# mLSTM cell and feed-forward on one core: the cell visits of two steps placed together in chunks 2 to 5

## The chip, the core and the metric

The kernel runs on one core of a Trainium2 chip. The metric is the device time of one execution in microseconds (us). The profile is that of one further execution, with the start, length and cause of waiting of each instruction on each engine: PE is TensorE (matmuls), DVE is VectorE, ACT is ScalarE, POOL is GpSimd, SP is the queue that issues nearly all DMAs.

## What is computed

Inputs are q, k, v and an output gate of 4 batches, 8 heads, 768 time steps and 40 features, and two gates per time step. The recurrence over time, and the feed-forward block on its result, are:

```python
m_new = np.maximum(f_gate[:, :, t] + m, i_gate[:, :, t])
f_stab = np.exp(f_gate[:, :, t] + m - m_new)
i_stab = np.exp(i_gate[:, :, t] - m_new)
C = f_stab[:, :, None, None] * C + i_stab[:, :, None, None] * np.einsum('bhd,bhe->bhde', vt, kt)
n = f_stab[:, :, None] * n + i_stab[:, :, None] * kt
h_tilde = np.einsum('bhde,bhe->bhd', C, qt)
denom = np.maximum(np.abs(np.einsum('bhd,bhd->bh', n, qt)[:, :, None]), 1.0)
y[:, :, t] = o * h_tilde / denom          # o is the sigmoid of the output gate
...
h = x @ w_in                              # x: y as (3072 tokens, 320); w_in: 320 x 2048
g = np.maximum(0.01 * h, h)
out = g @ w_out                           # w_out: 2048 x 320
```

All data are fp32 in the kernel.

## The kernel before

**Tiling.** Time is cut into 6 chunks of 128 time steps (`NB`). A *step* `s` is one chunk of one batch, all 8 heads: `s = 4c + b`, 24 steps in all. Inside a step the chunk is computed in closed form as two sub-chunks of 64 time steps: products of k and q, weighted by exponentials of the gates (`w`), plus the contribution of the state that the earlier sub-chunk left. The feed-forward block of chunk `c-1` (512 tokens of the four batches) runs while the cell of chunk `c` is computed.

**Feed-forward units.** `ff_units(g)` (L734) gives 32 units for a chunk. Units 0 to 15 are eight pairs `j` of *first* and *second* (L753, L757): 6 and then 4 matmuls into two PSUM tiles `ph`, 64x128 weights on 512 tokens; *second* ends with two relus on ScalarE (L748), which write `acts`. Units 16 to 31 are `part(n, m)` (L771): 4 matmuls into `po`; every fourth unit ends with a copy of `po` on ScalarE (L783) and a DMA to the output. `ph` and `po` share one PSUM pool, `psf`, of four buffers (tag `mm`), so two pairs `j` can be open at once. The profile counts an fp32 matmul as two records.

**Cell visits.** In chunks 2 to 5 a step has two visits on TensorE. `u_parts(s)` (L579) runs what is left of the step's exponentials, then the joint products `sd` of k with q and of k with the values (L595, L600) into two PSUM tiles; VectorE multiplies them by `w` (L605) and adds to the state (L577). `u_mix(s)` (L665) starts with the gate's tanh on ScalarE (L475), then multiplies state and values with the weighted products into `pT` (L676). Behind it GpSimd scales the state (L573), VectorE transposes `pT` (L683), forms denominators (L614 to L616) and gates (L687), GpSimd divides (L690), VectorE adds to the state (L577) and transposes to `x` (L694), and four DMAs write `x` to DRAM (L697). `gather_x(s)` (L700) later reads it back as `xT`, the input of the next chunk's `ph`. `sd`, `pT` and the gate transposes `tg` (`u_gates`, L796) share the PSUM pool `psc`, four buffers (tag `c`).

**Preparation.** `ahead(s)` (L814) registers the step's eight exponentials in `lazy` (`prep_exp`, L433; each masks out the future in place, in `w`), queues transposes of k and q and a product with a gate factor on VectorE (`prep_kq`, L481: L486, L492), issues ten DMAs of step `s+2` on SP (`rb`, L382; `ea`, L405), and queues on GpSimd the state's scaling (L573), `vu` (L459) and the mask of step `s+1` (`prep_mask`, L429: L431), which adds minus infinity to the future entries of `w` and must come before that step's exponentials. For chunk 1, `ahead` also has TensorE transposes (`u_split`).

**The order of the work.** It is written out by hand: TensorE, VectorE, ScalarE and GpSimd execute in the order in which the code calls (`tc.manual_schedule`, L915); only SP's queue is ordered by the compiler. In the loop over a chunk's units (L940), each turn first runs three exponentials of every step in `lazy`, then the feed-forward unit `i`, then the cell units that are due:

```python
upto = sum(p <= i for p in place) if c == 1 else min(n_c, (i + 1) * n_c // (n_ff - 8))
while done < upto:
    fn, s = cells[done]
    fn(s)
    ...
    if fn in ((u_mix, u_plain) if s < 2 * B - 1 else (u_parts,)):
        ahead(s + 1)
```

In chunks 2 to 4 (nine cell units) this places `u_parts` and `u_mix` of the four steps in turn behind units 2, 5, 7, 10, 13, 15, then the gates of the next chunk behind unit 18, and the last step behind units 21 and 23. In chunk 5 (eight cell units) they stand behind units 2, 5, 8, 11, 14, 17, 20 and 23. `ahead(s+1)` follows `u_parts(s)` from step 7 on. Gathers are held back to unit 15, since `xT` has one buffer. Behind a `u_mix`, the feed of later steps is issued on SP: the gate of step `s+2`, and k, v and `w` of step `s+4` (L974 to L976).

In chunk 1 (`place`, L931) the steps have `u_plain` (L637) in place of `u_mix`, `u_x` (L714) puts `x` into `xT` by TensorE transposes and five ScalarE copies each, and the weights are still being narrowed from 64 bits by VectorE and ScalarE (`narrow_weights`).

Of the kernel before, what the change touches and what calls it, by code (L numbers as in the profile page):

```python
# [18 lines left out]
def kernel(  # L19
# [27 lines left out]
    B, H, S, D = q.shape  # L47
# [3 lines left out]
    NS = B * NB  # L51
# [86 lines left out]
    def subs(s):  # L138

        for u in range(2):  # L140
            yield u, ts(u, SL), slice(SL * (1 - u), SL * (1 - u) + D)
# [78 lines left out]
    def narrow_weights(n):  # L220

        if not wide:
            return
        raw, dst = raws.pop(n)
        words = raw.bitcast(U32).rearrange("p (c two) -> p c two", two=2)
        lo, hi = words[:, :, 0], words[:, :, 1]
        d = dst.bitcast(U32)
        low, top = lo.bitcast(F32), hi.bitcast(F32)  # L230
        nc.scalar.activation(dst, top, AF.Abs)
        yield
        nc.vector.tensor_scalar(
            dst, dst, scalar1=2.0**-15, scalar2=122879.9921875, op0=ALU.max, op1=ALU.min,
        )
        yield
        nc.vector.tensor_scalar(
            d, d, scalar1=0x07FFFFFF, scalar2=3, op0=ALU.bitwise_and, op1=ALU.logical_shift_left,
        )
        yield  # L240
        nc.vector.scalar_tensor_tensor(d, in0=hi, scalar=0xC0000000, in1=d, op0=ALU.bitwise_and, op1=ALU.bitwise_or)  # L241
        yield
        nc.vector.tensor_scalar(hi, d, scalar1=0xFF800000, scalar2=None, op0=ALU.bitwise_and)  # L243
        yield
        nc.vector.scalar_tensor_tensor(low, in0=lo, scalar=2.0**-52, in1=top, op0=ALU.mult, op1=ALU.mult)  # L245
        yield
        nc.vector.tensor_tensor(dst, dst, low, op=ALU.add)  # L247
# [108 lines left out]
    def natural(s, i):  # L356

        t = rb_t[s % NR][:, i]
        return t[:, : H * D].rearrange("p (h d) -> p h d", d=D)

    def load_late(s, i):

        if B <= s < 2 * B:
            if i > 0:
                c, b = divmod(s, B)
                nc.sync.dma_start(natural(s, i), (k, q, o_gate)[i][b, :, ts(c, P), :].rearrange("h p d -> p h d"))
        elif s < NS:
            load_blocks(s, i)
# [58 lines left out]
                )  # L427

    def prep_mask(s):  # L429
        w = st[s]["w"]  # L430
        nc.gpsimd.tensor_tensor(w, w, cm2.unsqueeze(1).to_broadcast([P, H, SL]), op=ALU.add)  # L431

    def prep_exp(s):  # L433

        c, b = divmod(s, B)
        w = st[s]["w"]
        for h in range(H):
            bh = b * H + h
            yield nc.scalar.activation(w[:, h, :], w[:, h, :], AF.Exp, bias=gT[c][:, 0, bh : bh + 1], scale=1.0)  # L439
# [23 lines left out]
    def prep_qs(s):  # L463

        c, b = divmod(s, B)
        d = st[s]
        d["qs"] = wk.tile([P, Dm], F32, name="y")[:].rearrange("p (h d) -> p h d", d=D)
        nc.gpsimd.tensor_tensor(
            d["qs"], natural(s, 1), gT[c][:, 2, ts(b, H)].unsqueeze(2).to_broadcast([P, H, D]), op=ALU.mult,
        )  # L470
# [10 lines left out]
    def prep_kq(s):  # L481

        d = st[s]
        d["kqT"] = wk.tile([P, 2, PR * P], F32, name="kqT")
        for i in range(2):
            nc.vector.transpose(  # L486
                d["kqT"][:, i].rearrange("p (h t n) -> p h n t", n=TS, t=QW),
                raw_blocks(s, i, QW).rearrange("p (h n) d -> p h n d", n=TS),
            )
        for r in range(2):  # L490
            rows = ts(r, SL)
            nc.vector.tensor_tensor(  # L492
                mixed(s)[rows, 1 - r], d["kqT"][rows, 1].rearrange("p (h t) -> p h t", t=SL), d["ea"][rows], op=ALU.mult,
            )
# [10 lines left out]
    def u_split(s):  # L505

        d = st[s]
        d["kqT"] = wk.tile([P, 2, PR * P], F32, name="kqT")
        src = (d["k"], natural(s, 1))
        bank = [psc.tile([P, H, SL], F32, name=f"tk{r}", tag="c") for r in range(2)]  # L510
        for h in range(H):
            for i in range(2):
                for u, toks, rows in subs(s):
                    out_rows = rows if i == 0 else slice(SL * u, SL * u + D)
                    nc.tensor.matmul(
                        bank[u][out_rows, h, :], lhsT=src[i][toks, h, :D], rhs=ident[toks, toks], start=True, stop=True,
                    )
        for i in range(2):
            for u, toks, rows in subs(s):
                out_rows = rows if i == 0 else slice(SL * u, SL * u + D)  # L520
                nc.scalar.copy(d["kqT"][rows, i].rearrange("p (h t) -> p h t", t=SL), bank[u][out_rows])
# [275 lines left out]
        gates_T(c, bus.pop(c)[0])  # L797

    def cell_units(c):
        units = [(fn, c * B + n) for n in range(B) for fn in (u_parts, u_mix if c > 1 else u_plain)]  # L800
        if c + 1 < NB:
            units.insert(2 * B - 2, (u_gates, c + 1))
        if c == 1:
            units += [(u_x, s) for s in range(B, 2 * B)]
        return units

    lazy = {}

# [5 lines left out]
    def ahead(s):  # L814

        if s < NS:
            if s < 2 * B:
                u_split(s)
            lazy[s] = prep_exp(s)
            if s < 2 * B:  # L820
                prep_qs(s)
            else:
                prep_kq(s)
            if s + NR < NS:
                load_late(s + NR, 0)
                load_late(s + NR, 1)
                if s + NR >= 2 * B:
                    spread_q(s + NR)
            state_next(s, 0)
            prep_vu(s)  # L830
            if s + 1 < NS:
                prep_mask(s + 1)

    def feed(s):
        load(s)
        spread(s)
# [78 lines left out]
    with tc.manual_schedule(engines={E.PE, E.DVE, E.Activation, E.Pool}):  # L915
        ffs = first_chunk()
        for s in (B, B + 1):
            feed(s)
            for i in range(1, 3):
                load_late(s, i)  # L920
            if s == B:
                load_weights(3)
        for n in range(3):
            load_weights(QN + n)
        for s in (B + 2, B + 3):
            feed(s)


        ffs = ffs[2:]
        fetch = {4: (3, 4), 8: (5, 6), 15: (7,)}  # L930
        place = (2, 5, 7, 10, 12, 15, 16, 18, 21, 22, 24, 26, 28)  # L931
        now = (None for n in range(2, QN + NF // 2) for _ in narrow_weights(n))
        for c in range(1, NB + 1):
            if c > 1:
                ffs = ff_units(c - 1)
            cells = cell_units(c) if c < NB else []
            n_ff, n_c = len(ffs), len(cells)
            done = fed = 0
            waiting = []
            for i in range(n_ff):  # L940
                if c == 1:
                    run(now, 2 if i < 10 else 3 if i < 14 else 4)
                    for n in fetch.get(i, ()):
                        load_weights(QN + n)
                    if i == 0:
                        prep_mask(B)
                        ahead(B)
                        load_fi(3)
                for steps in lazy.values():
                    run(steps, 3)  # L950
                ffs[i]()
                if c + 1 < NB:
                    if i == (1 if c == 1 else 0):
                        gates(c + 1)
                    if i == (3 if c == 1 else 2):
                        gates_exp(c + 1)
                upto = sum(p <= i for p in place) if c == 1 else min(n_c, (i + 1) * n_c // (n_ff - 8))
                while done < upto:
                    fn, s = cells[done]
                    fn(s)  # L960
                    done += 1
                    if fn is u_mix:
                        waiting.append(s)
                    if fn in ((u_mix, u_plain) if s < 2 * B - 1 else (u_parts,)):
                        ahead(s + 1)
                if i >= n_ff // 2 - 1:
                    for s in waiting:
                        gather_x(s)
                    waiting.clear()
                while fed < done:  # L970
                    fn, s = cells[fed]
                    fed += 1
                    if fn in (u_mix, u_plain):
                        load_late(s + NR, 2)  # L974
                        if s + NL < NS:
                            feed(s + NL)  # L976
# [31 lines left out]
```

## Time and profile before

| | |
|---|---|
| median of 3 runs | 534.39 us (533.99 to 534.42) |
| the profiled execution's own time | 533.48 us |
| its span, first to last instruction | 531.7 us |
| mean granted TensorE clock | 0.98 of full speed |
| busy, share of the span: PE, PEld | 97%, 63% |
| busy: DVE, ACT, POOL | 45%, 32%, 21% |
| L740 `ph`: records, busy | 1120, 217.3 us |
| L775 `po`: records, busy | 768, 213.3 us |
| L595 and L600 `sd`: busy | 23.0 and 20.6 us (they overlap) |
| L676 `pT`: records, busy | 512, 18.4 us |
| L439 exponentials on ACT: count, busy | 192, 52.5 us |
| L431 masks on POOL: count, mean | 20, 1333 ns |

How to read it: busy time of TensorE is modelled and overlapping, so the order and start times of its pieces say more than the sums. The *chain of work* is followed back from the last instruction; each piece in it is what the next one waited for. A timeline line gives start (us from the span's beginning), length (us), engine, line, operation, output and inputs, shapes, count; in brackets, the idle time in front of it and what ended that. Times of GpSimd are rough.

### The profile page before, as it was taken

To read this page: it belongs to the slowest core of one execution; us is meant where nothing else is said; L and a number is where in the kernel's file an instruction comes from. 1 tells how busy PE (TensorE), PEld (TensorE's weight loads), DVE (VectorE), ACT (ScalarE), POOL (GpSimd) and SP (SyncE) were. 2 spreads that over 40 slices of the span, in tenths; PEclk is the share of its full clock that TensorE was granted. 3 is DMA by queue.
4 is the path that set the end of the run, shared out by engine and by line. 5 is a ranking of instruction groups with operands and counts; after the bars stand their busy time and mean duration, and the time that the engine had idled before them with its cause. 6 is when DMAs were issued, how large, how long until landed. Compare 5 with 4: busy or idle time off the path is not lost.

```text
span 531.7 us, 11350 instructions
## 1 busy us (share of the span) xinstructions
PE 517.3 (97%) x4501; PEld 334.5 (63%) x4501; DVE 241.1 (45%) x431; ACT 168.0 (32%) x458; POOL 111.1 (21%) x145
## 2 busy tenths in 40 slices
PE   7879989999999999999999999999999999999997
PEld 7767878667545577545577555577555577544675
DVE  4788998999055526055616055614054432000000
ACT  4566767515434311134311134311134300122100
POOL 4245254153022223022223012323011100000000
PEclk9768999999999999999999999999999999999999
DMA  9977677878745647555547555546531221000000
GB/s 116 161 205 161 146 185 183 185 143 175 157 92 114 125 121 162 120 119 112 125 132 146 131 114 102 130 136 151 123 73 39 66 71 43 32 1 0 14 12 25
DMA packets 165284, 59.13 MB, mean 111 GB/s; under 512 B 128816, under 2 KB 156016, under 8 KB 165232
## 3 DMA queue, kind: packets, MB, share of 16 engines
q1 hardware_dynamic: 164848, 58.28, 50.2%
q8 instruction: 35, 0.57, 0.4%
q10 hardware_dynamic: 384, 0.13, 0.1%
q14 instruction: 17, 0.14, 0.1%
HBM read 51.68 MB, written 6.70 MB: 110 GB/s over the span
## 4 chain that ended last, share of the span: by engine, by line
PE 81%; DVE 7%; SPq 6%; DMA 2%; ACT 2%; issue 1%; POOL 1%; ACTq 0%; DVEq 0%; POOLq 0%
PE po L775 36%; PE ph L740 36%; PE pT L676 3%; SPq L213 3%; PE sd L595 3%; SPq L338 2%; DVE raw L245 1%; SPq L352 1%; PE sd L600 1%; DVE qn L605 1%; DVE w_out L247 1%; DMA rb<-in_q_dram 1%; DVE w_out L241 1%; DVE raw L243 1%; DMA raw<-in_moe_w_in_dram 1%
## 5 line engine op out<-in xcount | busy, mean ns | idle before, releaser
L740 PE MATMUL ph<-xT,w_in 64*128 64x512 f32 (+1 forms) x1120 | 217.3, 538 | 0.6 <-ACT acts L748 0.6
L775 PE MATMUL po<-w_out,acts 128*128 128x320 f32 x768 | 213.3, 435 | 0.0
L775 PEld LDWEIGHTS po<-w_out,acts 128*128 128x128 f32 x768 | 143.8, 190 | 59.7 <-issue 1.8
L740 PEld LDWEIGHTS ph<-xT,w_in 64*128 64x128 f32 x1120 | 107.1, 189 | 91.1 <-issue 84.4
L748 ACT ACTIVATE acts<-ph 128x512 f32<-128x512 f32 (+1 forms) x112 | 53.9, 534 | 145.6 <-PE ph L740 145.5
L605 DVE TENSOR_TENSOR qn<-w,sd 64x512 f32<-64x512 f32 x40 | 27.4, 686 | 125.6 <-PE sd L600 90.1
L573 POOL TENSOR_TENSOR S<-S,f 40x336 f32<-40x336 f32 x36 | 30.7, 854 | 187.8 <-PE pT L676 146.8
L439 ACT ACTIVATE w<-w,gT 128x64 f32<-128x64 f32 (+1 forms) x192 | 52.5, 351 | 1.0 <-DVE w L425 1.0
L783 ACT COPY y<-po 128x320 f32<-128x320 f32 x12 | 5.1, 426 | 86.6 <-PE po L775 86.6
L783 ACT COPY hn<-po 128x320 f32<-128x320 f32 x12 | 5.1, 427 | 86.3 <-PE po L775 86.3
L690 POOL TENSOR_TENSOR xb<-xb,den 128x320 f32<-128x320 f32 x16 | 11.7, 729 | 88.9 <-DVE xb L687 88.9
L431 POOL TENSOR_TENSOR w<-w,i 128x512 f32<-128x512 f32 x20 | 26.7, 1333 | 10.2 <-DMA w<-a_dr 10.1
L683 DVE STREAM_TRANSPOSE hb<-pT 128x512 f32<-128x512 f32 x16 | 11.5, 717 | 38.1 <-PE pT L676 38.1
L595 PEld LDWEIGHTS sd<-kqT 40*64 40x64 f32 x640 | 20.3, 135 | 10.8 <-issue 9.3
L595 PE MATMUL sd<-kqT 40*64 40x64 f32 x640 | 23.0, 221 | 0.0
L492 DVE TENSOR_TENSOR qn<-kqT,ea 64x512 f32<-64x512 f32 x32 | 22.4, 701 | 1.1
L676 PEld LDWEIGHTS pT<-qn,S 128*64 128x64 f32 x512 | 16.2, 138 | 10.5 <-issue 6.9
L600 PE MATMUL sd<-S,vu 64*40 64x42 f32 x576 | 20.6, 215 | 0.7 <-POOL vu L459 0.7
L694 DVE STREAM_TRANSPOSE x<-xb 128x512 f32<-128x512 f32 x16 | 17.6, 1102 | 8.0 <-POOL xb L690 8.0
L486 DVE STREAM_TRANSPOSE kqT<-rb 128x512 f32<-128x512 f32 x32 | 20.7, 682 | 0.0
L600 PEld LDWEIGHTS sd<-S,vu 64*40 64x40 f32 x576 | 18.2, 111 | 0.8 <-POOL vu L459 0.8
L577 DVE TENSOR_TENSOR S<-S,sd 40x336 f32<-40x336 f32 x36 | 18.1, 503 | 0.9
(126 smaller groups left out, 369.1 us busy)
## 6 DMA issues: line engine op xcount, KB each, us to landing
w<-a_dr SPq DMA_DIRECT2D x40, 128.0 KB
rb<-in_k_dram SPq DMA_DIRECT2D x64, 80.0 KB
rb<-in_q_dram SPq DMA_DIRECT2D x64, 80.0 KB
rb<-in_o_gate_dram SPq DMA_DIRECT2D x64, 80.0 KB
ea<-a_dr SPq DMA_DIRECT2D x32, 128.0 KB
kn<-in_k_dram SPq DMA_DIRECT2D x24, 160.0 KB
raw<-in_moe_w_out_dram SPq DMA_DIRECT2D x6, 640.0 KB
S<-in_v_dram SPq DMA_DIRECT2D x80, 40.0 KB
```

The costliest lines, as they stand in the source:

```text
L431: nc.gpsimd.tensor_tensor(w, w, cm2.unsqueeze(1).to_broadcast([P, H, SL]), op=ALU.add)
L439: yield nc.scalar.activation(w[:, h, :], w[:, h, :], AF.Exp, bias=gT[c][:, 0, bh : bh + 1], scale=1.0)
L486: nc.vector.transpose(d["kqT"][:, i].rearrange("p (h t n) -> p h n t", n=TS, t=QW), raw_blocks(s, i, QW).rearrange("p (h n) d -> p h n d", ...
L492: nc.vector.tensor_tensor(mixed(s)[rows, 1 - r], d["kqT"][rows, 1].rearrange("p (h t) -> p h t", t=SL), d["ea"][rows], op=ALU.mult,)
L573: nc.gpsimd.tensor_tensor(new, old, g, op=ALU.mult)
L595: nc.tensor.matmul(bank[1 - u][toks, h, :], lhsT=kqT[rows, 0, ts(h, SL)], rhs=kqT[rows, 1, ts(h, SL)], start=True, stop=True,)
L600: nc.tensor.matmul(dC[u][:, h].rearrange("p k d -> p (k d)"), lhsT=d["ku"][toks, h], rhs=S_v[s % NL][toks, u, h, :, :V1], start=True, stop ...
L605: nc.vector.tensor_tensor(mixed(s)[toks, u], w[toks], bank[1 - u][toks], op=ALU.mult)
L676: nc.tensor.matmul(pT[DP * r : DP * (r + 1), j * P + u * SL : j * P + (u + 1) * SL], lhsT=S[:, u, h, :], rhs=m[:, u, h, :], start=True, st ...
L740: nc.tensor.matmul(ph[r][:, cols], lhsT=w_row(r, slot, j), rhs=xT[DP * r : DP * (r + 1), slot, cols], start=(slot == 0), stop=(slot == KC ...
L748: nc.scalar.activation(acts[:, f, cols], ph[r][:, cols], AF.Prelu, alpha=0.01)
L775: nc.tensor.matmul(po[n][:], lhsT=acts[:, f, ts(n, P)], rhs=w_out[:, f, :], start=(f == 0), stop=(f == NF - 1),)
```

## The change

In chunks 2 to 5 the order of the cell units becomes `u_parts(s)`, `u_parts(s+1)`, `u_mix(s)`, `u_mix(s+1)` for two steps at a time. A hand-written list places them: the first pair's parts behind unit 2 and its mixes behind unit 6, the second pair's parts behind unit 14, and gates and the second pair's mixes behind unit 19. `ahead(s+2)` now follows each `u_mix(s)` (and `ahead(9)` follows the last `u_plain` of chunk 1). From step 8 on the mask of a step is queued at the head of its own `ahead`, not at the tail of the `ahead` before. Chunk 1's own order of units stays.

```diff
     def prep_mask(s):
+        if s in masked:
+            return
+        masked.add(s)
         w = st[s]["w"]
...
     def cell_units(c):
-        units = [(fn, c * B + n) for n in range(B) for fn in (u_parts, u_mix if c > 1 else u_plain)]
+        if c == 1:
+            units = [(fn, c * B + n) for n in range(B) for fn in (u_parts, u_plain)]
+            units.insert(2 * B - 2, (u_gates, c + 1))
+            return units + [(u_x, s) for s in range(B, 2 * B)]
+        units = [(fn, c * B + n + m) for n in range(0, B, 2) for fn in (u_parts, u_mix) for m in range(2)]
         if c + 1 < NB:
             units.insert(2 * B - 2, (u_gates, c + 1))
-        if c == 1:
-            units += [(u_x, s) for s in range(B, 2 * B)]
         return units
...
             if s < 2 * B:
                 u_split(s)
+            if s > B:
+                prep_mask(s)
             lazy[s] = prep_exp(s)
...
             state_next(s, 0)
             prep_vu(s)
-            if s + 1 < NS:
+            if s + 1 < 2 * B:
                 prep_mask(s + 1)
...
+        pairs = (2, 2, 6, 6, 14, 14, 19, 19, 19)
...
-                upto = sum(p <= i for p in place) if c == 1 else min(n_c, (i + 1) * n_c // (n_ff - 8))
+                upto = min(n_c, sum(p <= i for p in (place if c == 1 else pairs)))
...
-                    if fn in ((u_mix, u_plain) if s < 2 * B - 1 else (u_parts,)):
+                    if fn is u_plain and s < 2 * B - 1 or fn is u_parts and s == 2 * B - 1:
                         ahead(s + 1)
+                    elif fn is u_mix or fn is u_plain:
+                        ahead(s + 2)
```

More of the change, by code (lines that the diff above doesn't have):

```diff
@@ L799, in cell_units @@
     def cell_units(c):
-        units = [(fn, c * B + n) for n in range(B) for fn in (u_parts, u_mix if c > 1 else u_plain)]
+        if c == 1:
[3 more added lines that the diff above has]
+        units = [(fn, c * B + n + m) for n in range(0, B, 2) for fn in (u_parts, u_mix) for m in range(2)]
         if c + 1 < NB:
             units.insert(2 * B - 2, (u_gates, c + 1))
-        if c == 1:
-            units += [(u_x, s) for s in range(B, 2 * B)]
         return units
+    masked = set()
     lazy = {}
```

## The prediction

> **What bounds the kernel now.** I read the page's chain of work first, then the chain in order of time, then the timelines of the four engines around one visit.
>
> ```profile
> PE 81%; DVE 7%; SPq 6%; DMA 2%; ACT 2%; issue 1%; POOL 1%; ACTq 0%; DVEq 0%; POOLq 0%
> PE po L775 36%; PE ph L740 36%; PE pT L676 3%; SPq L213 3%; PE sd L595 3%; SPq L338 2%; DVE raw L245 1%; SPq L352 1%; PE sd L600 1%; DVE qn L605 1%; DVE w_out L247 1%; DMA rb<-in_q_dram 1%; DVE w_out L241 1%; DVE raw L243 1%; DMA raw<-in_moe_w_in_dram 1%
> ```
>
> TensorE sets the end; the other engines' parts of the chain lie in the first quarter. The chain from 180 to 290 us is TensorE alone. Its columns are start, length and what, with two records for one fp32 matmul:
>
> ```profile
> 227.82 6.21 PE ph L740 x28
> 234.03 1.08 PE pT L676 x32
> 235.11 4.49 PE ph L740 x20
> ```
>
> No gap stands between a feed-forward piece and a cell visit. Two piece lengths give a rate and a start cost: (6.21 - 4.49) / 8 = 0.215 us a record, and 6.21 - 28 x 0.215 = 0.19 us for every new start. The last chunk, with no visits, takes 34.53 us for its 160 ph records and 34.66 us for 128 po records, which is 69.2 us against 80.1 us for a chunk with visits (219.68 to 299.78).
>
> So TensorE has no slack at all, and two things matter: how many starts go away, and whether anything makes TensorE wait. For the second, here are VectorE, then GpSimd, then ScalarE around the visit above:
>
> ```profile
> 229.85 1.30 DVE L486 STREAM_TRANSPOSE kqT<-rb 128x512 f32<-128x512 f32 x2
> 231.19 1.41 DVE L492 TENSOR_TENSOR qn<-kqT,ea 64x512 f32<-64x512 f32 x2
> 235.16 0.72 DVE L683 STREAM_TRANSPOSE hb<-pT 128x512 f32<-128x512 f32 x1 [2.57 <-PE pT L676]
> ...
> 236.55 0.49 DVE L687 SCALAR_TENSOR_TENSOR xb<-rb,hb 128x320 f32<-128x320 f32 x1
> ...
> 237.95 1.10 DVE L694 STREAM_TRANSPOSE x<-xb 128x512 f32<-128x512 f32 x1 [0.37 <-POOL xb L690]
> ```
>
> ```profile
> 234.79 0.77 POOL L573 TENSOR_TENSOR S<-S,f 40x336 f32<-40x336 f32 x1 [26.66 <-PE pT L676]
> 237.18 0.73 POOL L690 TENSOR_TENSOR xb<-xb,den 128x320 f32<-128x320 f32 x1 [1.63 <-DVE xb L687]
> 237.99 0.77 POOL L573 TENSOR_TENSOR S<-S,f 40x336 f32<-40x336 f32 x1
> 238.83 0.72 POOL L459 TENSOR_TENSOR vu<-kn,gT 128x320 f32<-128x320 f32 x1
> 239.51 1.28 POOL L431 TENSOR_TENSOR w<-w,i 128x512 f32<-128x512 f32 x1
> ```
>
> ```profile
> 239.63 1.08 ACT L748 ACTIVATE acts<-ph 128x512 f32<-128x512 f32 x2 [4.13 <-PE ph L740]
> 240.60 1.54 ACT L439 ACTIVATE w<-w,gT 128x64 f32<-128x64 f32 x6
> ```
>
> Each engine's order is the code's order. The mask (L431) that GpSimd does here is that of a step whose exponentials (L439) come two visits later, so an exponential never waits for its mask, and a relu (L748) behind exponentials is late by their own length only. The relu matters, because ph has four PSUM buffers: the first half of pair j+2 needs those that the relu of pair j sets free. This wait does occur once:
>
> ```profile
> 55.76 2.70 PE L740 MATMUL ph<-xT,w_in 64*128 64x256 f32 x20 [0.56 <-ACT acts L748]
> ```
>
> **What the Trainium skill says.** "TensorEngine Tiling (Array Packing)", Key Properties: a change of tiling mode drains TensorE. The trace agrees: 0.19 us per start between ph (64x128), sd (40x64), pT (128x64) and po (128x128). "PSUM — Partial Sum Buffer", Engine vs sequencer instructions: the queues of ScalarE, VectorE and GpSimd are strictly first in, first out. The orders above agree, and the argument below rests on it. "TensorE: Matmul & The Clock Gate", Part 1: after about 3.4 us of idleness TensorE's clock falls to half, and some 3.4 us of work bring it back. No idle time of that length is in this trace after its start, so it is not shown; but at the start the clock is granted at 0.50 to 0.83 from 10 to 45 us, and the same 20 records of ph take 4.08 us at 39.78 and 2.43 us at 46.05.
>
> **The change part by part.** The sum is made against the profiled execution, 533.48 us with a span of 531.7 us; the median of the runs is 0.91 us above it.
>
> Fewer starts. An sd visit occupies 1.07 us plus the 0.19 us of the restart behind it; its 64 records run at about 0.059 us for four, 0.94 us. A second sd directly behind the first costs 0.94 instead of 1.26: 0.32 saved. A pT visit costs 1.27; its 32 records start 0.028 us apart, 0.90 us: 0.37 saved. Chunks 2 to 5 have 8 pairs of each: 8 x 0.69 = 5.5 us. The gate transposes (tg, in chunks 2 to 4) now stand before pT; their tile shape differs, so only one restart goes: 3 x 0.19 = 0.6. Together **-6.1 us**; at least the restarts alone (19 x 0.19 = 3.6), at most 6.6.
>
> Preparation moved. Before, ahead(s+1) followed u_parts(s), long ahead of the next mix. Now ahead(s+2) follows u_mix(s) and stands in front of u_mix(s+1) on every queue: on VectorE 2.75 us of transposes and products (L486, L492), on GpSimd mask 1.27, state 0.77, vu 0.72, on ScalarE eight exponentials, on SP ten loads. The mask has lost its lead: it is the first thing in ahead(s+2). Let t = 0 be the end of pT(s) (235.11 above) for the pair at unit 6:
> - VectorE ends L687 of s at 1.93 and x of s at 3.94, then L486/L492 for s+2 to 6.65, and only then serves s+1: L687 ends at 6.65 + 1.88 = 8.53.
> - GpSimd: xb of s ends at 2.80; mask, state and vu of s+2 and the state of s+1 run to 6.5; xb of s+1 must wait for 8.53, runs 8.67 to 9.40; then the mask of s+3, **9.48 to 10.75**.
> - ScalarE: unit 7 puts three exponentials of s+2 and three of s+3 ahead of the relu of j=3. The latter three wait for 10.75 and run to about 11.65; the relu's two tiles are done at 12.15 and 12.65.
> - TensorE: pT(s+1) to 0.9, then 28 records of units 7 to 9 (6.21): at 7.1 it wants the banks of j=3 for j=5, and gets them at about 12.2. It stops 5.1 us, 5.2 with the second bank.
> After that ScalarE has caught up: ten exponentials and the relu of j=4 end at 16.2, and j=6 begins at 16.7. So one stop for each of chunks 2 to 5: 4 x 5.2 = **+20.8 us**. The pair at unit 19 lies among po units. ScalarE has there only a copy every 8.6 us, and four banks: the same 10.75 us of waiting stay hidden, at no cost. Nor do the new pairs of sd wait: kqT of s+3 is done at 6.65 + 3.89 + 2.75 = 13.3, and unit 14 lies 17 us behind unit 6; L605 and the state additions of two steps (3.8 us) fit into the 8.6 us from unit 2 to unit 6. If GpSimd and VectorE hold each other up (L492 took 1.86 instead of 1.41 us at 120.82, beside a GpSimd operation of 1.26 instead of 0.77), the stop grows by up to 0.5.
>
> Chunk 1's end. ahead(9) now follows the last u_plain there. Its mask comes behind hn (GpSimd, to 130.71), so to about 132.1; three of its exponentials stand ahead of the xT copies, which had begun at 126.52. The 20 copies (1.65 us for five), 8 exponentials (2.15) and 4 y copies then end the last xT copy at about 142.1, where chunk 2 had started at 139.56: **+2.5 us**, from 0 to 4.
>
> Clock. Each of the four stops is longer than the skill's 3.4 us. For each I take what the trace shows for 20 ph records at a lowered clock, 4.08 - 2.43 = 1.65 us: **+6.6 us**. Bounds: nothing, if no idle window is whole, and 3.4 us a stop (6.8 us at half clock, an estimate from that page): 0 to 13.6.
>
> Banks and SP. sd of a pair fills all four psc banks; two are free again after L605, so pT(s) and pT(s+1) find room, and I cost it at nothing. If the second takes a bank that state_add(s) still reads, it waits to t = 2.4, some 1.6 us, at the four pairs of unit 19 (at unit 6 the stop hides it): 0 to 6. SP's issues of two steps come together: from the trace x 1.56, rb k and q 3.8, ea 1.1, xT 2.56 per step. Behind the x of s+1 at 10.6 the gathers are issued by about 22, TensorE needs xT at 27, and landing took under 3.3 us before (issue done 296.5, ph at 299.78): nothing, at worst 2 us at each of four chunk starts.
>
> Sum: 533.48 - 6.1 + 20.8 + 2.5 + 6.6 = 557.3, and 0.9 to the median: 558. Its own range is 549 (no clock loss, chunk 1 hidden) to 567.
>
> **The rivals.** *Faster:* the stop doesn't come. It decides at one point: the mask of s+3 must end by t = 5.2, so that six exponentials' remainder (0.8) and the relu (1.1) are done at 7.1. For it: the mask itself waits for no one and would fit into GpSimd's idle time if it were queued ahead of xb. Against: the code queues it behind. Then 533.5 - 6.1 + 0.9 = 528. *Half a stop:* exponentials of s+3 fall behind the relu, or VectorE is shorter than summed: 536 to 549. *More waits:* bank or gather waits on top: 558 + 6 + 6 = 570 (567 to 577).
>
> **How the numbers follow.** Forecast 0.68, faster 0.14, half a stop 0.08, more waits 0.10. What a measurement of this kernel can tell from no change is about 0.2%, 1 us. Leaving out the faster case and some of the top, the range is 540 to 569. Faster 0.15, same 0.02, slower 0.83.
>
> **What would show it.** Right: TensorE waits in chunks 2 to 5 for the relu (ph L740 by ACT acts L748), four times, about 5 us; ScalarE's exponentials wait for GpSimd's mask; GpSimd's xb waits for VectorE with L492 ahead of it; sd and pT runs of double length, some 0.3 us shorter than two. The clock below 1 behind each stop shows the last term. Wrong: no relu wait above 1 us, or chunks of 78 us.

## The result and the profile after

The changed kernel takes 563.51 us (median of 6, 560.69 to 567.88) against 534.19 us (median of 6, 533.67 to 535.04): a ratio of 1.0553, interval 1.0509 to 1.0598. Forecast were 558.0 us and a range of 540 to 569. The profiled execution took 567.88 us, the slowest of the six, with a span of 565.8 us against 531.7 before, and a mean granted clock of 0.955 against 0.98. Line numbers of the lines shown are 3 higher than before (L740 is L743, L748 is L751, L431 is L434).

TensorE's waits in the changed kernel (line, what it waited for, total us, times, longest):

```profile
PE ph L743 <- ACT acts L751: 22.4, 5, 5.7
PE ph L743 <- ACT xT L729: 2.8, 1, 2.8
```

Before, the first of these was 0.6 us, once. Four of the five are the forecast stops, one each in chunks 2 to 5. This is TensorE around the first pair of chunk 2:

```profile
162.70 2.08 PE L679 MATMUL pT<-qn,S 128*64 128x64 f32 x64
164.71 6.28 PE L743 MATMUL ph<-xT,w_in 64*128 64x512 f32 x28
176.63 13.96 PE L743 MATMUL ph<-xT,w_in 64*128 64x512 f32 x52 [5.64 <-ACT acts L751]
```

The two pT visits are one run of 64 records, and behind 28 records of ph TensorE stands still for 5.64 us. What it waited for can be followed back through ScalarE, GpSimd and VectorE of the same stretch:

```profile
167.91 0.83 ACT L442 ACTIVATE w<-w,gT 128x64 f32<-128x64 f32 x3 [5.88 <-POOL w L434]
175.28 0.83 ACT L442 ACTIVATE w<-w,gT 128x64 f32<-128x64 f32 x3 [6.54 <-POOL w L434]
176.01 1.06 ACT L751 ACTIVATE acts<-ph 128x512 f32<-128x512 f32 x2
```

```profile
166.60 1.27 POOL L434 TENSOR_TENSOR w<-w,i 128x512 f32<-128x512 f32 x1
...
173.29 0.72 POOL L693 TENSOR_TENSOR xb<-xb,den 128x320 f32<-128x320 f32 x1 [2.60 <-DVE xb L690]
173.97 1.27 POOL L434 TENSOR_TENSOR w<-w,i 128x512 f32<-128x512 f32 x1
```

```profile
168.94 2.29 DVE L495 TENSOR_TENSOR qn<-kqT,ea 64x512 f32<-64x512 f32 x2
...
172.66 0.49 DVE L690 SCALAR_TENSOR_TENSOR xb<-rb,hb 128x320 f32<-128x320 f32 x1
```

The relu runs at 176.01, because three exponentials stand in front of it; they run at 175.28, because their mask ended then; the mask began at 173.97, behind xb, which waited for VectorE's L690. The first pT had ended at about 163.8, so the mask ended 11.4 us behind it, where the prediction had 10.75.

Then the clock. Columns are the stretch, its length, TensorE's busy time and records, the granted clock, DMA share and GB/s:

```profile
172.00:174.00 2.00, 0.00 (x0) 1.00 0.76 165
174.00:176.00 2.00, 0.00 (x0) 0.61 0.64 141
176.00:178.00 2.00, 1.36 (x3) 0.50 0.50 128
178.00:180.00 2.00, 2.00 (x7) 0.50 0.78 169
180.00:182.00 2.00, 2.00 (x9) 0.68 0.67 147
182.00:184.00 2.00, 2.00 (x13) 1.00 0.57 195
```

It falls within the stop (170.99 to 176.63) and is back some 5 us behind its end. In between ph is slowed to little more than half its rate: 7 records from 178 to 180 instead of 12 or 13.

### The profile page after: what moved, and what is told of

Read it like the earlier page. It is cut to its first block, busy times and chain, and to the rows that moved or that the text cites. A ratio compares the mean times of both kernels' runs of the same rounds, so it can differ in the third digit from the quotient of the medians.

```text
span 565.8 us, 11340 instructions
## 1 busy us (share of the span) xinstructions
PE 527.1 (93%) x4501; PEld 361.6 (64%) x4501; DVE 243.8 (43%) x431; ACT 168.2 (30%) x458; POOL 113.0 (20%) x145
## 4 chain that ended last, share of the span: by engine, by line
PE 61%; issue 9%; DVE 8%; SPq 7%; DMA 6%; ACT 5%; POOL 4%; ACTq 0%; POOLq 0%; DVEq 0%
PE ph L743 28%; PE po L778 27%; PE sd L598 2%; PE pT L679 2%; DMA S<-in_v_dram 2%; SPq L338 2%; SPq L213 2%; POOL w L434 2%; ACT w L442 1%; DMA raw<-in_moe_w_out_dram 1%; SPq L352 1%; POOL xb L693 1%; DMA rb<-in_q_dram 1%; SPq L343 1%; DVE qn L495 1%
## 5 line engine op out<-in xcount | busy, mean ns | idle before, releaser
L743 PE MATMUL ph<-xT,w_in 64*128 64x512 f32 (+1 forms) x1120 | 229.6, 561 | 25.5 <-ACT acts L751 22.4
L743 PEld LDWEIGHTS ph<-xT,w_in 64*128 64x128 f32 x1120 | 134.0, 197 | 107.4 <-issue 65.5
L751 ACT ACTIVATE acts<-ph 128x512 f32<-128x512 f32 (+1 forms) x112 | 53.7, 531 | 138.3 <-PE ph L743 138.2
L576 POOL TENSOR_TENSOR S<-S,f 40x336 f32<-40x336 f32 x36 | 32.9, 913 | 201.3 <-PE pT L679 175.3
L495 DVE TENSOR_TENSOR qn<-kqT,ea 64x512 f32<-64x512 f32 x32 | 31.8, 995 | 0.9
L434 POOL TENSOR_TENSOR w<-w,i 128x512 f32<-128x512 f32 x20 | 26.5, 1325 | 11.0 <-ACT bu L295 9.0
L686 DVE STREAM_TRANSPOSE hb<-pT 128x512 f32<-128x512 f32 x16 | 11.4, 714 | 39.2 <-PE pT L679 39.0
L598 PE MATMUL sd<-kqT 40*64 40x64 f32 x640 | 21.4, 220 | 0.0
L489 DVE STREAM_TRANSPOSE kqT<-rb 128x512 f32<-128x512 f32 x32 | 20.3, 674 | 0.0
```

The lines of the kernel that those rows point to most:

```text
L489: nc.vector.transpose(d["kqT"][:, i].rearrange("p (h t n) -> p h n t", n=TS, t=QW), raw_blocks(s, i, QW).rearrange("p (h n) d -> p h n d", ...
L495: nc.vector.tensor_tensor(mixed(s)[rows, 1 - r], d["kqT"][rows, 1].rearrange("p (h t) -> p h t", t=SL), d["ea"][rows], op=ALU.mult,)
L576: nc.gpsimd.tensor_tensor(new, old, g, op=ALU.mult)
L598: nc.tensor.matmul(bank[1 - u][toks, h, :], lhsT=kqT[rows, 0, ts(h, SL)], rhs=kqT[rows, 1, ts(h, SL)], start=True, stop=True,)
L743: nc.tensor.matmul(ph[r][:, cols], lhsT=w_row(r, slot, j), rhs=xT[DP * r : DP * (r + 1), slot, cols], start=(slot == 0), stop=(slot == KC ...
L751: nc.scalar.activation(acts[:, f, cols], ph[r][:, cols], AF.Prelu, alpha=0.01)
```

## The experiments

The theory after the result was that of the prediction: the relu stands in ScalarE's queue behind exponentials whose mask comes last in GpSimd's. The rivals were the doubled number of exponentials in a turn, the joined visits themselves (waits for PSUM banks, restarts), and VectorE's preparation between the two mixes. Each time below stands beside the kernel before, run on the same chip (534.44 us for the first four experiments, 534.51 us for the other four).

### All masks early

```diff
-            if s + 1 < 2 * B:
+            if s + 1 < 2 * B + 2:
                 prep_mask(s + 1)
...
                     elif fn is u_mix or fn is u_plain:
                         ahead(s + 2)
+                    if fn is u_parts and c > 1 and s + 2 < NS:
+                        prep_mask(s + 2)
```

> Every mask gets its lead back: that of step s+2 is queued on GpSimd right behind u_parts(s), that of step 9 at the tail of ahead(8). The order of the visits stays as changed. Theory (the relu waits behind exponentials that wait for a mask): the four stops of 5.0 to 5.7 us before the first half of j=5 go, and with them the lowered clock behind each, and the 2.8 us at the start of chunk 2: 526 to 529 us, 5 to 8 below the kernel before. Rival A (six exponentials in a turn instead of three hold the relu up, mask or no mask): stops of 1 us or more stay in chunks 2 to 5, 535 us or more. Rival B (the joined visits themselves cost TensorE, by banks or restarts): no stop, but chunks no shorter than 80 us, 533 us or more.

Measured: 530.39 us, ratio 0.9925 (0.9896 to 0.9955). No wait of TensorE is left in chunks 2 to 5, and the 2.8 us at the start of chunk 2 are gone too. The same joined visits, with the masks' lead given back, are faster than the kernel before. This is chunk 3 from the first piece of its chain to that of chunk 4, with its first pair of pT visits:

```profile
220.34 7.07 PE ph L743 x32
238.21 2.02 PE pT L679 x64
299.16 7.07 PE ph L743 x32
```

Chunks 2 to 4 take 78.8 us against 80.1, chunk 5 takes 78.0 against 79.4. The two pT visits take 2.02 us where two of 1.08 us and a start of 0.19 stood, 0.33 less. Six exponentials in a turn hold nothing up when their masks are there, and the joined visits cost TensorE nothing. The time is 1.4 us above what was expected. At the first long run of ph the profiled execution was already 2.7 us behind that of the third experiment (42.20 against 39.49 us at the 20 records of ph). Up to there the two kernels run the same instructions in the same order on every engine, so the edit doesn't explain this part; whether the other three executions have it is not known.

### Exponentials of one step after the other

```diff
-                for steps in lazy.values():
-                    run(steps, 3)
+                left = 3
+                for steps in lazy.values():
+                    while left and next(steps, steps) is not steps:
+                        left -= 1
```

> The masks stay late as changed; only ScalarE's order is altered: three exponentials in a turn in all, first those of step s+2, then those of s+3. Theory: the relu of j=3 has no late mask in front of it any more. The first exponential of s+3 now stands ahead of the relu of j=4; the mask ended 11.4 us behind pT(s) in the changed kernel, so that relu's first tile is done at about 12.3, where TensorE wants it at 11.5: stops of 0.8 us instead of 5.6, no lowered clock in chunks 2 to 5; the start of chunk 2 stays late. 535 to 538 us. Rival (VectorE's or GpSimd's lateness itself holds TensorE, not ScalarE's order): stops stay near 5 us, above 555 us.

Measured: 534.99 us, ratio 1.0013 (0.9999 to 1.0028). The stops are 0.9 us in chunks 2 to 4 and 0.3 in chunk 5, against 5.0 to 5.7. The mask is as late as in the changed kernel: at the first pair of chunk 2 it ends 10.54 us behind the start of the ph run that follows pT, there 10.53. So the lateness of GpSimd and VectorE reached TensorE through the order of ScalarE's queue. The time is at the lower edge of what was expected; the start of chunk 2 waited only 0.8 us in the profiled execution.

### Masks early from step 10 on

The second half of the first experiment's diff alone.

> As the run with all masks early, but the mask of step 9 stays late, so the end of chunk 1 stays as changed. Theory: the stops and the lowered clock of chunks 2 to 5 go (22.0 + 11.4 us of the changed kernel), the late start of chunk 2 stays (2.8 us of waiting, 1.8 of lowered clock): 530 to 532 us, 4 to 5 above the run with all masks early. Rival (the late start of chunk 2 comes from ahead(9)'s work on VectorE and ScalarE, not from its mask): no difference between the two runs.

Measured: 529.97 us, ratio 0.9927 (0.9901 to 0.9952). The four stops are gone. TensorE still waits 1.7 us for xT at the start of chunk 2, where the first experiment doesn't wait at all. All six kernels whose mask of step 9 is late wait there, 0.7 to 2.8 us, and the three whose mask is early (the first experiment and the last two) don't. So that wait does come from the mask of step 9, but its size differs between executions: the fifth experiment has the order of the changed kernel up to there and waits 0.7 us, not 2.8. The first experiment was expected to be 4 to 5 us faster than this run, and was not: the two medians agree within 0.5 us, as the rival had it. In the profiled executions the wait was shorter than the 2.8 us of the changed kernel, the clock was not lowered behind it (32 records of ph in 7.14 us), and the first experiment lost 2.7 us at the start, as said. By the totals alone, the question would be open; the waits answer it.

### The mask behind vu

```diff
-            if s + 1 < 2 * B:
+            if s + 1 < 2 * B or s >= 2 * B + 2 and s % 2 == 0 and s + 1 < NS:
                 prep_mask(s + 1)
```

> A dose between: the mask of s+3 is queued at the tail of ahead(s+2), behind the state and vu of s+2, so ahead of xb of s+1. By the timeline of the changed kernel it then ends about 7.0 us behind pT(s) instead of 11.4. Theory: relu tiles at 8.5 and 9.0 against TensorE's 7.1: four stops of 1.4 to 1.8 us, too short to lower the clock; start of chunk 2 late as changed; 537 to 541 us. Rival (the stop isn't set by when the mask ends): stops unlike 1.6 us, either none or near 5.

Measured: 540.14 us, ratio 1.0108 (1.0063 to 1.0154). The profiled execution (538.62 us) has stops of 1.5, 1.6, 1.6 and 1.9 us, and no lowered clock behind them. These are TensorE and the mask at the first pair of chunk 2:

```profile
160.00 6.28 PE L743 MATMUL ph<-xT,w_in 64*128 64x512 f32 x28
167.86 11.91 PE L743 MATMUL ph<-xT,w_in 64*128 64x512 f32 x52 [1.58 <-ACT acts L751]
164.76 1.71 POOL L434 TENSOR_TENSOR w<-w,i 128x512 f32<-128x512 f32 x1
```

The same 52 records took 13.96 us in the changed kernel. Even 11.91 is 0.54 more than 52 x 0.215 + 0.19. That fits the second bank (the PSUM buffer of the pair's second ph tile), which the second relu sets free half a microsecond behind the first.

### The mask a bit later

```diff
+            if s >= 2 * B + 2 and s % 2 == 0:
+                prep_ku(s)
             if s + 1 < 2 * B or s >= 2 * B + 2 and s % 2 == 0 and s + 1 < NS:
                 prep_mask(s + 1)
```

`prep_ku` is the GpSimd product of `prep_vu`, on the same tile.

> As the run with the mask behind vu, with one more GpSimd product (vu of s+2 written once more with the same values, 0.72 us) in front of that mask. Theory: the four stops grow from 1.65 us by 0.75 to about 2.4 us. Open is the clock: after stops of up to 1.9 us it was not lowered, after the 2.84 us at the start of chunk 2 in the changed kernel it was. If it holds at 2.4 us: 542 to 545 us. If it falls, 1.8 to 3.4 us more behind each stop: 549 to 557 us. Rival (stops not set by the mask's end): unchanged 540 us.

Measured: 548.92 us, ratio 1.0267 (1.0245 to 1.0288), stops of 2.65 to 3.07 us. They grew by more than the 0.75 us expected, and as the mask did: at the first pair of chunk 2 the stop is 1.14 us longer than in the run before, and the mask ends 1.14 us later behind the start of the ph run (160.91 here). The clock held behind two of the stops and fell behind the other two (ph is L751 in this kernel, the relu L759):

```profile
169.91 11.91 PE L751 MATMUL ph<-xT,w_in 64*128 64x512 f32 x52 [2.72 <-ACT acts L759]
166.81 1.71 POOL L434 TENSOR_TENSOR w<-w,i 128x512 f32<-128x512 f32 x1
...
334.74 13.60 PE L751 MATMUL ph<-xT,w_in 64*128 64x512 f32 x52 [3.07 <-ACT acts L759]
...
418.60 14.86 PE L751 MATMUL ph<-xT,w_in 64*128 64x512 f32 x52 [2.65 <-ACT acts L759]
```

A stop of 2.65 us cost 2.95 us more through the clock (14.86 against 11.91), one of 2.72 us nothing. So at this size the length of a stop doesn't alone decide. The time lies just below the range for a clock that falls each time, and above that for one that holds.

### The preparation behind both mixes

```diff
-                    elif fn is u_mix or fn is u_plain:
+                    elif fn is u_plain:
                         ahead(s + 2)
+                    elif fn is u_mix and s % 2:
+                        ahead(s + 1)
+                        ahead(s + 2)
```

> As changed, but the ahead of both steps of a pair stands behind both mixes, so VectorE's 2.75 to 3.6 us of L489 and L495 no longer stand between the two mixes. Theory (what counts is that the mask of s+3 is the last but two in GpSimd's queue, behind everything of the pair): xb of s+1 ends 6.7 us behind pT(s), then mask, state and vu of s+2 take 2.8 more, and the mask of s+3 still ends at about 10.8: stops of about 5.0 us with a lowered clock, 557 to 565 us. Rival (VectorE's preparation between the mixes is the cause): the mask ends 2.75 to 3.6 us earlier, stops of 2.0 to 2.9 us, below 552 us.

Measured: 564.09 us, ratio 1.0545 (1.052 to 1.057), the same as the changed kernel; stops of 5.1 to 5.8 us. GpSimd at the first pair of chunk 2:

```profile
167.62 0.73 POOL L693 TENSOR_TENSOR xb<-xb,den 128x320 f32<-128x320 f32 x1 [2.35 <-DMA rb<-in_o_gate_dram]
168.30 1.27 POOL L434 TENSOR_TENSOR w<-w,i 128x512 f32<-128x512 f32 x1
169.65 0.76 POOL L576 TENSOR_TENSOR S<-S,f 40x336 f32<-40x336 f32 x1
170.49 0.72 POOL L462 TENSOR_TENSOR vu<-kn,gT 128x320 f32<-128x320 f32 x1
171.17 1.71 POOL L434 TENSOR_TENSOR w<-w,i 128x512 f32<-128x512 f32 x1
```

xb of s+1 is done at 168.35, 6.7 us behind the first pT; in the changed kernel it was 10.2 us. (The wait named ahead of it is the latest that the profile knows of; VectorE's L690 had ended at 167.47.) But mask, state and vu of s+2 then come in front of the mask of s+3, which ends at 172.9, 11.3 us behind pT. Taking VectorE's work out of the way gains nothing as long as the mask stays last in the queue.

### Two versions that go further

The all-early kernel with `pairs = (2, 2, 6, 6, 15, 15, 19, 19, 19)`:

> As the run with all masks early, with the second pair's parts behind unit 15 instead of 14. By the pieces of TensorE's chain a chunk has 6 feed-forward pieces there against 10 before: 4 starts fewer a chunk, not the 4.75 of the prediction, because the border between ph and po at unit 15, which a visit used to cover, now costs a start of its own. With the visit at that border: a start of 0.19 us fewer in each of 4 chunks, chunks of 78.6 instead of 78.8 us, 529 to 530.5 us. Rival (a start at a change from ph to po costs nothing): chunks stay at 78.8.

Measured: 528.52 us, ratio 0.9881 (0.9862 to 0.9899), half a microsecond below the expected range. Chunks 3 and 4 take 78.6 us (78.8 with the parts at 14) and chunk 5 77.8 (78.0); chunk 2 is hardly shorter, 78.75 against 78.81. These are the pieces of the chain in chunk 3:

```profile
217.94 7.07 PE ph L743 x32
227.03 8.78 PE ph L743 x40
237.82 19.09 PE ph L743 x88
258.97 8.81 PE po L778 x32
270.48 26.04 PE po L778 x96
```

Five feed-forward pieces stand where there were ten before, and the border from ph to po lies under the visit between 237.82 + 19.09 and 258.97.

The same with the first pair's parts of chunks 3 to 5 at the end of the chunk before:

```diff
+            if 2 <= c < NB - 1:
+                for s in (B * c + B, B * c + B + 1):
+                    u_parts(s)
+                    prep_mask(s + 2)
```

(the loop over a chunk's cell units then starts at the third of them in chunks 3 to 5)

> As the run with parts behind unit 15, and the first pair's parts of chunks 3 to 5 stand at the very end of the chunk before, so that the border between po and ph is covered by a visit too: one start of 0.19 us fewer at three borders, chunks of 78.4 us, 528 to 530 us. Rival: parts so early wait for the exponentials or the masks (a wait of TensorE or VectorE at the border), 530 us or more.

Measured: 529.21 us, ratio 0.9891 (0.9874 to 0.9909), no new wait. Chunk 4 takes 78.43 us there and 78.56 in the run before it, chunk 3 78.62 and 78.58. A gain of 0.2 us at a border is at the edge of what these traces show, and not in the totals.

## Why the prediction was right, and where its sizes were off

The mechanism and its place were right, point by point: four stops at j=5 in chunks 2 to 5, caused by exponentials that wait for a mask behind xb; the pair at unit 19 without a stop; the late start of chunk 2; a lowered clock behind each stop; no wait for PSUM banks by pT, and none for the gathers. The experiments confirm the cause from three sides: the mask early (no stop), ScalarE's order altered (0.9 us at most), and the mask in between (stops of 1.65 and 2.8 us on average, the longer one for the later mask). The stop even follows the mask one for one. At the first pair of chunk 2 the mask of s+3 ends 6.47, 7.61, 10.39 and 10.53 us behind the start of the ph run that follows pT (fourth, fifth and sixth experiment, changed kernel), and the stops there are 1.58, 2.72, 5.50 and 5.64 us, each 4.89 us less. The faster case failed at the point named for it: it needed the mask within 5.2 us, and the mask came at 11.4. Given that lead, it does come true, at 530.39 instead of the 528 worked out.

The terms of the sum, in the profiled executions. That of the changed kernel is the slowest of its six, so the sum is above the 29.3 us by which the medians differ:

| term | forecast | measured | how measured |
|---|---|---|---|
| fewer starts | -6.1 | -5.3 | 80.1 to 78.8 us in chunks 2 to 4, 79.4 to 78.0 in chunk 5, with all masks early |
| four stops | +20.8 | +24.9 | 22.0 of waiting, and 4 x 0.73: a new start (0.19) and the second bank (0.54) |
| start of chunk 2 | +2.5 | +3.6 | 139.49 to 143.09, 2.8 of it the wait for xT |
| clock | +6.6 | +10.9 | 52 ph records against 11.91: 2.05 + 2.81 + 1.49 + 2.84; 32 at the start of chunk 2: 8.83 - 7.14 = 1.69 |
| sum | +23.8 | +34.1 | span: 565.8 - 531.7 = 34.1 |

Three terms were mis-sized.
- **Clock.** The prediction took 1.65 us a stop, from 20 records early in the trace. After a stop it is 2.3 us on average, and the start of chunk 2, which had been given none, pays 1.69. "TensorE: Matmul & The Clock Gate", Part 1, has the clock fall after some 3.4 us of idleness; here it fell with stops of 2.65, 2.84 and 3.07 us, and held behind others of 2.72, 2.73 and 2.84. The measurement decides: shorter stops are not safe. Whether this term also makes the kernel uneven is not shown. Its six times spread over 7.2 us, where the kernel before spreads over 1.4; but those of the third experiment, which in its profiled execution has no lowered clock behind a stop, spread over 6.9.
- **Stops.** The mask was 0.65 us later than summed. L495 alone took 0.88 more, 2.29 us instead of 1.41 beside GpSimd's products; the rest went a little faster than summed. The prediction had allowed 0.5 for it, outside the sum. "SBUF — State Buffer", Who interferes with whom, says that a VectorE instruction with two inputs in SBUF contends with a GpSimd instruction that reads SBUF. The trace agrees: L495, with two inputs, is longer beside GpSimd's products, and L489 (L486 before), with one, takes 1.27 us beside them and took 1.30 alone. No run here separates the ports from other causes. The second bank's wait had been put at 0.1; it was 0.54. And a stop cuts a run of ph in two: the start of the second part, 0.19 us, was left out.
- **Starts.** The step "19 x" counted one start for each visit that goes. It left out that in chunks 2 to 4 the visit of the third step used to stand exactly at the border from ph to po, where TensorE changes its tile shape in any case. With nothing in between, the border has a start of its own: 4 a chunk are saved, not 4.75 on average. This is 0.6 us of the 0.8 that are missing. The run with the parts at unit 15 gets about 0.2 us a chunk back in chunks 3 to 5.

What stays open: what the other 0.8 of the 3.6 us at the start of chunk 2 is (TensorE also waits 1.0 us for VectorE's narrowing of `w_out` in chunk 1, which no run took apart), and which terms are smaller in the executions nearer to the median, of which no trace was kept.

## What to carry to other kernels

When a preparation step is moved behind the work of another step, follow each of its instructions in each in-order queue up to the first consumer that the bound engine needs: here a 1.3 us mask on an engine that is idle for four fifths of the time cost 5.6 us of TensorE, by way of exponentials that merely stood ahead of a relu. Joining small visits is worth one start each (about 0.2 to 0.35 us), and only if the borders that the visits used to cover don't come back as starts. Price a stop of a matmul-bound kernel with the clock behind it: behind the four stops of 5.0 to 5.7 us it cost 9.2 us on top of 22.0.

## What the runs showed that was not expected

A stop of TensorE of 2.65 us was followed by a clock of 0.50 to 0.56 for 6 us, one of 2.72 us by full clock, in the same execution. The same holds between executions. At the start of chunk 2 TensorE stops for 2.84 us both in the changed kernel and in the sixth experiment. The 32 records behind it take 8.83 us in the one and 7.14, as at full clock, in the other:

```profile
142.56 7.14 PE L743 MATMUL ph<-xT,w_in 64*128 64x512 f32 x32 [2.84 <-ACT xT L729]
```

And the clock can fall when TensorE is already at work again. In the fifth experiment the stop of 3.07 us ended at 334.74, and the clock was full up to 336:

```profile
334.00:336.00 2.00, 1.26 (x5) 1.00 0.76 164
336.00:338.00 2.00, 2.00 (x8) 0.58 0.49 162
```

VectorE's L495 (two products on 64 partitions) took 1.41 us alone and 1.8 to 2.8 us where GpSimd ran its own products beside it, while GpSimd's mask took 1.71 instead of 1.27: both sides lengthen.
